# Scores of a pair in one stretch of three couples, with the norm steps of later groups half a group sooner

## The chip, the cores and the metric

The kernel runs on one core of a Trainium2 chip. The metric is the device time of one launch in microseconds (us). A program on one core is compared here by the median of several runs, beside one profiled execution.

## The reference

Attention with RMS-normed queries and keys for 8 batches of 12 heads, 448 tokens and 64 channels a head, followed by a token mixer of rank 32 and a feed-forward block of 768 to 3072 to 768 channels.

```python
q_n, k_n = rmsnorm(q, g_q), rmsnorm(k, g_k)              # over the 64 channels
scores = q_n @ k_n.T / 8                                 # 448 x 448 for each head
attn = softmax(scores)
x = attn @ v                                             # heads side by side: 448 x 768
u = x + (x.T @ U @ V).T                                  # U 448 x 32, V 32 x 448
out = u + relu(u @ w_ch1) @ w_ch2
```

## The kernel before

**Units.** Two heads make a pair, and each batch has six pairs. Two pairs make a group `gi`; there are 24 groups, three to a batch. In a group the first pair is `a == 0` and the second is `a == 1`; `pr` is the pair's number in its batch, and `pairs[i]` lists all 48.

**Norm of a group.** `load` brings q, k and v to SBUF (SP's queue). `squares` (ScalarE, or GpSimd for the early groups) and `sums` (VectorE, two reductions) give the sums of squares; `roots` (ScalarE, lines 169 and 170, `Ln` and `Exp`) gives the factors; `scale_dma` (GpSimd) multiplies, and `values` (GpSimd) casts v. `roots`, the scaling and `values` together are `scale_all`. From group 6 on (`DMA_FROM`, the third batch, as batches count from 0) `turn_dma` turns q and k by four DMA transposes on SP's queue, and `take_dma` multiplies the turned q by the gains on GpSimd (line 386). The buffer of the turned groups is double.

**Scores of a pair.** `Sc(b, pr, r)` with r = 0, 1, 2 computes 128 keys for both heads of the pair: two matmuls that contract 64 rows each, one in the upper and one in the lower half of the array, which run side by side (a couple). Their results are two PSUM banks of one tile of the pool `ps_sc` (2 tiles of 2 banks). r = 3 takes the last 64 keys of both heads in one matmul over 128 rows, whose result is a tile of the pool `ps` (4 tiles of one bank). ScalarE's `Exp` (line 416) takes each result to `E`, of which there are two. `Srows` issues several of them back to back, which is called a stretch here. From the third batch a group had three stretches of two couples: (0, 1) of its first pair; (2) of the first and (0) of the second, then r = 3 of the first; (1, 2) of the second, then r = 3.

**Values of a pair.** `V(b, pr, half)` multiplies `E` by v into a tile `pv` of the pool `ps`; VectorE divides by the sum (lines 444 and 445).

**Mixer and feed-forward.** `mix_t`, `mix_tr` and eight `mix_rows` for each batch; then 24 `up` pieces (6 matmuls each, line 529, emptied by ScalarE's `Relu`, line 536), then `down` in parts of 6 matmuls (line 561); four parts fill one tile `po`, which VectorE empties (line 571). All of these take their PSUM tile from the pool `ps` too, so `ps` serves `ph1`, `po`, `pv`, `pu`, `pw`, `pm` and r = 3 of the scores.

**Order.** The order on every engine is the order in which the program issues, and it is written out by a planner. It has two lists: `att` (attention pieces, each with a cost) and `mlp` (mixer and feed-forward pieces, each with a cost; `up` 1.14, a `down` part 0.98). `ca` and `cm` are the costs issued so far. An attention piece is issued once `ca` is not above `due(cm)`, which is linear in pieces; otherwise the next `mlp` piece is issued:

```python
take_att = ia < len(att) and (not may_mlp or ca <= due(cm) and ready(*att[ia][1:]))
return a_two + (a_all - a_two) * (c - SECOND) / (m_end - m_one - SECOND)
```

So a step of cost 0 (`squares`, `sums`, `scale_all`, `turn_dma`, `take_dma`, `load`) is issued together with the next step behind it that costs something, and not with the one ahead of it. `m_one` is the cost of the `mlp` list up to its first piece of the second batch.

Of the kernel before, what the change touches and what calls it, by code (L numbers as in the profile page):

```python
# [9 lines left out]
FP32 = mybir.dt.float32  # L10
BF16 = mybir.dt.bfloat16
AX = mybir.AxisListType.X
AF = mybir.ActivationFunctionType
# [6 lines left out]
DMA_FROM = 6  # L20
# [6 lines left out]
def kernel(  # L27
# [13 lines left out]
    nc = tc.nc  # L41
    B, H, S, D = q.shape
# [4 lines left out]
    P = 128  # L47
    NT = S // 64
    NJ = S // P
    SM = NJ * P  # L50
# [8 lines left out]
    NPAIR = H // 2  # L59
    HALF = dm // 2  # L60
    scal = 1.0 / (D ** 0.5)
# [6 lines left out]
    ep = ctx.enter_context(tc.tile_pool(name="ep", bufs=2))  # L68
    xp = ctx.enter_context(tc.tile_pool(name="xp", bufs=3))
    outp = ctx.enter_context(tc.tile_pool(name="outp", bufs=3))  # L70
    ps_sc = ctx.enter_context(tc.tile_pool(name="ps_sc", bufs=2, space=bass.MemoryType.PSUM))
    ps = ctx.enter_context(tc.tile_pool(name="ps", bufs=4, space=bass.MemoryType.PSUM))


    groups = []
# [183 lines left out]
    bias = gg[:, 1:2]  # L259
# [77 lines left out]
    at = {"pe": 0.0, "act": 0.0, "dve": 0.0}  # L337
    exp_done = {}

    def runs(eng, us):  # L340
        at[eng] = us + (at["pe"] if eng == "pe" else max(at["pe"], at[eng]))

    qk, es, xs = {}, {}, {}
# [57 lines left out]
    NB = 2 * NJ + 1  # L401

    def Sc(b, pr, r):
        qT, kT = qk[divmod(b * NPAIR + pr, 2)]
        if r == 0:
            es[(b, pr)] = ep.tile([P, NB, S], BF16, name="E", tag="E")
        n = min(2, NB - 2 * r)
        if r < NJ or b == 0:
            sc = ps_sc.tile([P, 2, 512], FP32, name="sc", tag="sc")
        else:  # L410
            sc = ps.tile([P, 1, 512], FP32, name="sl", tag="ps")
        keys = slice(r * P, (r + 1) * P)
        for i in range(n):
            d = slice(i * D, (i + 1) * D) if r < NJ else slice(0, P)
            nc.tensor.matmul(sc[:, i, :S], kT[d, keys], qT[d], start=True, stop=True)  # L415
        nc.scalar.activation(es[(b, pr)][:, 2 * r:2 * r + n, :], sc[:, :n, :S], AF.Exp, scale=scal, bias=bias)  # L416
        runs("pe", 0.25)
        runs("act", 0.9 if n == 2 else 0.52)
        exp_done[(b, pr)] = at["act"]

    def Srows(blocks):
        for x in blocks:
            Sc(*x)
# [158 lines left out]
    pairs = [(b, pr) for b in range(B) for pr in range(NPAIR)]  # L582
    att = []

    def add_att(cost, f, *a):
        att.append((cost, f, a))
# [58 lines left out]
    for i, (b, pr) in enumerate(pairs):  # L645
        if b == 0:
            continue
        gi, a = divmod(i, 2)
        more = gi + 1 < len(groups)
        by_dma = gi + 1 >= DMA_FROM  # L650
        soon = gi + 2 < len(groups)

        if a == 0:
            if pr == 0 and b > 1:
                add_att(0.5, V, *pairs[i - 1], 0)
                add_att(0.5, V, *pairs[i - 1], 1)
            add_att(0.45, Srows, ((b, pr, 0), (b, pr, 1)))
            if gi == DMA_FROM:
                add_att(0.0, sums, gi + 1, 0)
                add_att(0.0, sums, gi + 1, 1)  # L660
                add_att(0.0, load, gi + 2)
            if by_dma and more and gi >= DMA_FROM:
                add_att(0.0, scale_all, gi + 1)
            if b == 1 and pr == 0:
                add_att(0.8, lambda: None)
            if not by_dma:
                add_att(0.0, squares, gi + 1, 0, nc.gpsimd)
                add_att(0.0, squares, gi + 1, 1, nc.gpsimd)
                if gi + 2 < DMA_FROM:
                    add_att(0.0, load, gi + 3)  # L670
            if pr != 0:
                add_att(0.4, V, *pairs[i - 1], 0)
                add_att(0.5, V, *pairs[i - 1], 1)
            if gi < DMA_FROM:
                add_att(0.0, sums, gi + 1, 0)
                add_att(0.0, sums, gi + 1, 1)
            add_att(1.0, Srows, ((b, pr, 2), (b, pr + 1, 0), (b, pr, 3)))
            if more and gi + 1 > DMA_FROM:
                add_att(0.0, turn_dma, gi + 1)
                add_att(0.0, take_dma, gi + 1)  # L680
                if gi + 3 < len(groups):
                    add_att(0.0, load, gi + 3)
            if gi < DMA_FROM:
                add_att(0.0, scale_all, gi + 1)
            if gi + 2 == DMA_FROM:
                add_att(0.0, squares, gi + 2, 0, nc.gpsimd)
                add_att(0.0, squares, gi + 2, 1, nc.gpsimd)
                add_att(0.0, weights, 2)
            add_att(0.4, V, b, pr, 0)
        else:  # L690
            add_att(0.6, Srows, ((b, pr, 1), (b, pr, 2), (b, pr, 3)))
            if not by_dma:
                add_att(0.5, V, *pairs[i - 1], 1)
                add_att(0.39, T, gi + 1, 0)
                add_att(0.39, T, gi + 1, 1)
                continue
            if gi + 1 == DMA_FROM:
                add_att(0.5, V, *pairs[i - 1], 1)
                add_att(0.0, turn_dma, gi + 1)
                add_att(0.0, load, gi + 2)  # L700
                add_att(0.0, take_dma, gi + 1)
                add_att(0.0, squares, gi + 2, 0, nc.gpsimd)
                add_att(0.0, squares, gi + 2, 1, nc.gpsimd)
                continue
            if soon:
                add_att(0.0, squares, gi + 2, 0)
                add_att(0.0, squares, gi + 2, 1)
            add_att(0.5, V, *pairs[i - 1], 1)
            if soon:
                add_att(0.0, sums, gi + 2, 0)  # L710
                add_att(0.0, sums, gi + 2, 1)
    add_att(0.55, V, *pairs[-1], 0)
    add_att(0.55, V, *pairs[-1], 1)

# [9 lines left out]
    for b in range(B):  # L724
# [14 lines left out]
        tiles = [(col, half) for col in cols for half in range(2)]  # L739
# [81 lines left out]
    while ia < len(att) or im < len(mlp):  # L821
# [8 lines left out]
        if take_att:  # L830
            c, f, a = att[ia]
# [11 lines left out]
        else:  # L843
            c, f, a, _ = mlp[im]
# [34 lines left out]
```

## Time and profile before

| what | value |
|---|---|
| median of 3 runs (lowest, highest) | 591.55 us (589.73, 592.12) |
| own time of the profiled execution | 590.86 us |
| its span | 589.0 us |
| TensorE matmul busy | 575.1 us, 4825 instructions |
| ScalarE busy | 300.2 us |
| VectorE busy | 197.1 us |
| GpSimd busy | 213.8 us |
| `Exp` of a couple, 128x896 | 1003 ns, x144 |
| `Exp` of r = 3, 128x448 | 638 ns, x42 |
| `Relu` of an `up`, 128x448 | 548 ns |
| one reduction of `sums` | 1079 ns |

The profiled execution took 1.9 us more than its span and 0.7 us less than the median. In a row of the timeline, the first number is the start in us from the span's start, the second how long the group of instructions took from its first start to its last end; matmuls overlap, so the distance from one start to the next is what TensorE spends. What stands in square brackets is idle time of that engine ahead of the row, and what ended it.

### The profile page before, as it was taken

What the parts mean: (1) busy time and instruction counts of PE and PEld (TensorE: products, weight loads), DVE (VectorE), ACT (ScalarE), POOL (GpSimd) and SP (SyncE); (2) the same over time, 40 slices, a digit from 0 to 9 for tenths busy, and PEclk for the clock granted to TensorE, in tenths of its full rate; (3) what the DMA queues carried; (4) which work ended last, traced back from release to release, by engine and by line L of the source; (5) the groups of instructions that cost most, each with busy time, mean ns of one, the idle gap of its engine ahead of it and who ended that gap; (6) DMA issues with size and microseconds to landing.
All of it is one profiled execution on the core that took longest, in us unless ns stands there. A gap on an engine that the chain in (4) does not pass through costs nothing.

```text
span 589.0 us, 11701 instructions
## 1 busy us (share of the span) xinstructions
PE 575.1 (98%) x4825; PEld 335.0 (57%) x4826; DVE 197.1 (33%) x458; ACT 300.2 (51%) x472; POOL 213.8 (36%) x312
## 2 busy tenths in 40 slices
PE   8899999989999999999999999999999999999996
PEld 7555556545665555555566555665556655655563
DVE  6576655312344223521244320631134310410011
ACT  6866750668453774466753568347753254014200
POOL 4995684373144434415054605333352000000000
PEclk9999999999999999999999999999999999999999
DMA  8799997773636651674166732567014210420022
GB/s 217 164 241 241 241 200 186 180 170 99 145 67 165 156 127 18 169 198 107 22 155 100 190 96 37 158 161 155 9 37 105 48 28 1 61 67 1 1 53 55
DMA packets 104509, 68.21 MB, mean 116 GB/s; under 512 B 66568, under 2 KB 101256, under 8 KB 104456
## 3 DMA queue, kind: packets, MB, share of 16 engines
q1 hardware_dynamic: 95044, 58.03, 41.7%
q0 software_dynamic: 9408, 9.44, 9.6%
q8 instruction: 38, 0.62, 0.4%
q14 instruction: 15, 0.12, 0.1%
q10 hardware_dynamic: 4, 0.00, 0.0%
HBM read 52.20 MB, written 11.01 MB: 107 GB/s over the span
## 4 chain that ended last, share of the span: by engine, by line
PE 91%; DMA 3%; SPq 1%; POOL 1%; ACT 1%; issue 1%; DVE 1%; POOLq 0%; ACTq 0%
PE po L561 36%; PE ph L529 36%; PE pv L441 6%; PE sc L415 5%; PE sl L415 2%; PE pv L437 2%; DMA qf<-in_q_dram 2%; PE pm L512 2%; ACT E L416 1%; DMA vf<-in_v_dram 1%; PE pu L460 1%; DMA qT<-qn 1%; PE pt L354 1%; POOL kp L174 1%; SPq L100 0%
## 5 line engine op out<-in xcount | busy, mean ns | idle before, releaser
L561 PE MATMUL po<-w2b,hT 128*128 128x384 bf16 x1344 | 237.7, 326 | 0.0
L529 PE MATMUL ph<-uT,w1b 128*128 128x448 bf16 x1140 | 229.4, 352 | 0.0
L416 ACT ACTIVATE E<-sc,gg 128x896 bf16<-128x896 f32 (+1 forms) x150 | 140.1, 988 | 119.5 <-PE sc L415 119.2
L561 PEld LDWEIGHTS <-hT 128*128 128x128 bf16 x1344 | 125.9, 98 | 77.0 <-issue 3.3
L529 PEld LDWEIGHTS <-w1b 128*128 128x128 bf16 x1140 | 107.9, 98 | 95.1 <-issue 3.0
L536 ACT ACTIVATE hT<-ph 128x448 bf16<-128x448 f32 x184 | 98.4, 548 | 122.7 <-PE ph L529 121.9
L444 DVE RECIPROCAL r<-pv 128x4 f32<-128x4 f32 x96 | 17.4, 182 | 185.8 <-PE pv L441 185.6
L193 POOL TENSOR_TENSOR qn<-qf,rs 128x384 bf16<-128x384 f32 x36 | 29.9, 830 | 136.9 <-ACT rs L170 136.9
L386 POOL TENSOR_SCALAR qT<-qT,gg 128x448 bf16<-128x448 bf16 x36 | 50.5, 1402 | 73.1 <-DMA qT<-qn 54.3
L571 DVE TENSOR_TENSOR ob<-po,x 128x384 f32<-128x384 f32 x48 | 26.8, 558 | 103.3 <-PE po L561 103.1
L441 PE MATMUL pv<-va,E 128*128 128x65 bf16 x1152 | 57.1, 194 | 0.0
L441 PEld LDWEIGHTS <-E 128*128 128x128 bf16 x1152 | 50.5, 98 | 6.4
L415 PE MATMUL sc<-qT,kT 64*128 64x448 bf16 (+1 forms) x294 | 43.3, 354 | 5.9 <-ACT E L416 3.0
L162 DVE TENSOR_REDUCE ssq<-sq 128x14 f32<-128x896 f32 x45 | 46.9, 1079 | 3.7 <-ACT sq L140 3.6
L437 PE MATMUL pv<-vl,E 128*128 128x130 bf16 x192 | 42.2, 220 | 0.3 <-ACT E L416 0.2
L445 DVE TENSOR_TENSOR x<-pv,r 128x256 bf16<-128x256 f32 x96 | 40.7, 424 | 3.3
L415 PEld LDWEIGHTS <-kT 64*128 64x128 bf16 (+1 forms) x336 | 14.1, 94 | 44.4 <-issue 38.2
L517 DVE TENSOR_TENSOR x<-pm,x 128x384 bf16<-128x384 f32 x48 | 26.3, 554 | 17.3 <-PE pm L512 15.0
L193 POOL TENSOR_TENSOR kp<-kf,rs 128x384 bf16<-128x384 f32 x36 | 29.8, 828 | 0.0
L416 ACT ACTIVATE E<-sl,gg 128x448 bf16<-128x448 f32 x42 | 26.8, 638 | 0.0
L437 PEld LDWEIGHTS <-E 128*128 128x128 bf16 x192 | 18.7, 97 | 9.8 <-issue 2.0
L571 DVE TENSOR_TENSOR ob<-po,u_rest 128x384 f32<-128x384 f32 x8 | 4.5, 558 | 46.9 <-PE po L561 46.9
(93 smaller groups left out, 323.5 us busy)
## 6 DMA issues: line engine op xcount, KB each, us to landing
qf<-in_q_dram SPq DMA_DIRECT2D x23, 448.0 KB, 3.6
kf<-in_k_dram SPq DMA_DIRECT2D x23, 448.0 KB, 4.8
out_dram<-ob SPq DMA_DIRECT2D x50, 192.0 KB, 2.7
vf<-in_v_dram SPq DMA_DIRECT2D x48, 192.0 KB, 5.3
w1b<-in_moe_w_ch_dram POOLq DMA_DIRECT2D x4, 1152.0 KB, 19.8
w2b<-in_moe_w_ch_dram POOLq DMA_DIRECT2D x8, 576.0 KB, 13.2
vf<-in_v_dram SPq DMA_DIRECT2D x48, 32.0 KB, 4.6
out_dram<-ob SPq DMA_DIRECT2D x12, 96.0 KB, 3.8
```

The lines of the kernel that those rows point to most:

```text
L162: nc.vector.tensor_reduce(ssqs[gi][:, i, :], sqs.pop((gi, i)), AX, ALU.add)
L193: nc.gpsimd.tensor_tensor(main.rearrange("p (t i) d -> p i t d", i=2), src[:, c, :2 * NJ].rearrange("p (i t) d -> p i t d", i=2), rs[:, c, ...
L386: nc.gpsimd.tensor_scalar(qT[:, a], qT[:, a], gg[:, 0:1], None, ALU.mult)
L415: nc.tensor.matmul(sc[:, i, :S], kT[d, keys], qT[d], start=True, stop=True)
L416: nc.scalar.activation(es[(b, pr)][:, 2 * r:2 * r + n, :], sc[:, :n, :S], AF.Exp, scale=scal, bias=bias)
L437: nc.tensor.matmul(pv[:, i].rearrange("p e d -> p (e d)"), E[:, 2 * NJ, w:w + P], vl[:, lp, :], start=True, stop=False)
L441: nc.tensor.matmul(pv[:, i, e, :], E[:, 2 * j + e, w:w + P], va[:, (first_h + step * e) * NJ + j, :], start=False, stop=(e == 1 and j == N ...
L445: nc.vector.tensor_tensor(xs[b].rearrange("p i (h d) -> p i h d", d=D)[:, 2 * half:2 * half + 2, h0:h0 + step + 1:step, :], pv[:, :, :, :D ...
L529: nc.tensor.matmul(ph, w1b[:, dt, ht * P:(ht + 1) * P], uT[:, dt, off:off + S], start=(dt == 0), stop=(dt == KD - 1))
L536: nc.scalar.activation(hT[:, ht, off:off + S], ph, AF.Relu)
L561: nc.tensor.matmul(po, hT[:, ht, col:col + P], w2b[:, ht, half * HALF:(half + 1) * HALF], start=(ht == 0), stop=(ht == KH - 1))
L571: nc.vector.tensor_tensor(ob[:, h], po, urows(b, col, half), ALU.add)
```

## The change

From group 6 on a pair's scores are issued by a new function, `Spair`, in one stretch: the couple r = 2 first, into two one-bank tiles of `ps`, then the couples 0 and 1 into the two tiles of `ps_sc`, then r = 3 into a third tile of `ps`. The results of r = 2 have an `Exp` each. A group so has two stretches of three couples where it had three of two. Each pair is now: `Spair`, then the two `V` of the pair before it (in a batch's first pair, these two `V` and then `Spair`).

The norm steps move as well. `squares` of group gi + 2 stay ahead of the second `V` in the second pair of group gi. `sums` of gi + 2 stay behind that `V`, and now `scale_all` of gi + 2 follows them there; before, it came in the next group behind its first stretch. `turn_dma`, `take_dma` and `load` come behind the group's first stretch and no longer behind its second. Around group 6 the load of group 7 moves from behind `turn_dma` of group 6 to the group before; the squares of group 7 go from GpSimd to ScalarE, ahead of `turn_dma` of group 6; its `sums` and `scale_all` come ahead of the last `V` of the second batch.

```diff
+    def Spair(b, pr):
+        qT, kT = qk[divmod(b * NPAIR + pr, 2)]
+        E = es[(b, pr)] = ep.tile([P, NB, S], BF16, name="E", tag="E")
+        ts = [ps.tile([P, 512], FP32, name="sl", tag="ps")[:, :S] for _ in range(2)]
+        for i in range(2):
+            d = slice(i * D, (i + 1) * D)
+            nc.tensor.matmul(ts[i], kT[d, 2 * P:3 * P], qT[d], start=True, stop=True)
+        for i in range(2):
+            nc.scalar.activation(E[:, 4 + i, :], ts[i], AF.Exp, scale=scal, bias=bias)
+        ...
+        tiles = [ps_sc.tile([P, 2, 512], FP32, name="sc", tag="sc") for _ in range(2)]
+        for r in range(2):
+            for i in range(2):
+                d = slice(i * D, (i + 1) * D)
+                nc.tensor.matmul(tiles[r][:, i, :S], kT[d, r * P:(r + 1) * P], qT[d], start=True, stop=True)
+        last = ps.tile([P, 512], FP32, name="sl", tag="ps")[:, :S]
+        nc.tensor.matmul(last, kT[:, SM:], qT, start=True, stop=True)
+        nc.scalar.activation(E[:, 6, :], last, AF.Exp, scale=scal, bias=bias)
+        for r in range(2):
+            nc.scalar.activation(E[:, 2 * r:2 * r + 2, :], tiles[r][:, :, :S], AF.Exp, scale=scal, bias=bias)
...
+        if a == 0 and pr == 0 and b > 1:
+            add_att(0.5, V, *pairs[i - 1], 0)
             if gi == DMA_FROM:
                 add_att(0.0, sums, gi + 1, 0)
                 add_att(0.0, sums, gi + 1, 1)
-                add_att(0.0, load, gi + 2)
-            if by_dma and more and gi >= DMA_FROM:
                 add_att(0.0, scale_all, gi + 1)
+            add_att(0.5, V, *pairs[i - 1], 1)
+        if gi >= DMA_FROM:
+            add_att(1.0, Spair, b, pr)
+            if a == 0 and more:
+                add_att(0.0, turn_dma, gi + 1)
+                add_att(0.0, take_dma, gi + 1)
+                if gi + 3 < len(groups):
+                    add_att(0.0, load, gi + 3)
+            if pr != 0:
+                add_att(0.45, V, *pairs[i - 1], 0)
+                if a == 1 and soon:
+                    add_att(0.0, squares, gi + 2, 0)
+                    add_att(0.0, squares, gi + 2, 1)
+                add_att(0.45, V, *pairs[i - 1], 1)
+                if a == 1 and soon:
+                    add_att(0.0, sums, gi + 2, 0)
+                    add_att(0.0, sums, gi + 2, 1)
+                    add_att(0.0, scale_all, gi + 2)
+            continue
...
             add_att(0.6, Srows, ((b, pr, 1), (b, pr, 2), (b, pr, 3)))
+            if gi + 2 == DMA_FROM:
+                add_att(0.0, load, gi + 3)
...
-            if gi + 1 == DMA_FROM:
-                add_att(0.5, V, *pairs[i - 1], 1)
-                add_att(0.0, turn_dma, gi + 1)
-                add_att(0.0, load, gi + 2)
-                add_att(0.0, take_dma, gi + 1)
-                add_att(0.0, squares, gi + 2, 0, nc.gpsimd)
-                add_att(0.0, squares, gi + 2, 1, nc.gpsimd)
-                continue
...
+            add_att(0.0, squares, gi + 2, 0)
+            add_att(0.0, squares, gi + 2, 1)
             add_att(0.5, V, *pairs[i - 1], 1)
...
+            add_att(0.0, turn_dma, gi + 1)
+            add_att(0.0, take_dma, gi + 1)
+            add_att(0.0, load, gi + 3)
```

More of the change, by code (lines that the diff above doesn't have):

```diff
@@ L419, in Sc @@
         exp_done[(b, pr)] = at["act"]
+    def Spair(b, pr):
[7 more added lines that the diff above has]
+            nc.scalar.activation(E[:, 4 + i, :], ts[i], AF.Exp, scale=scal, bias=bias)
+        runs("pe", 0.4)
+        runs("act", 1.04)
+        tiles = [ps_sc.tile([P, 2, 512], FP32, name="sc", tag="sc") for _ in range(2)]
[8 more added lines that the diff above has]
+            nc.scalar.activation(E[:, 2 * r:2 * r + 2, :], tiles[r][:, :, :S], AF.Exp, scale=scal, bias=bias)
+        runs("pe", 0.6)
+        runs("act", 2.3)
+        exp_done[(b, pr)] = at["act"]
     def Srows(blocks):
@@ L651 @@
         soon = gi + 2 < len(groups)
-        if a == 0:
-            if pr == 0 and b > 1:
-                add_att(0.5, V, *pairs[i - 1], 0)
-                add_att(0.5, V, *pairs[i - 1], 1)
-            add_att(0.45, Srows, ((b, pr, 0), (b, pr, 1)))
+        if a == 0 and pr == 0 and b > 1:
+            add_att(0.5, V, *pairs[i - 1], 0)
             if gi == DMA_FROM:
@@ L660 @@
                 add_att(0.0, sums, gi + 1, 1)
-                add_att(0.0, load, gi + 2)
-            if by_dma and more and gi >= DMA_FROM:
                 add_att(0.0, scale_all, gi + 1)
-            if b == 1 and pr == 0:
+            add_att(0.5, V, *pairs[i - 1], 1)
[17 more added lines that the diff above has]
+            continue
+        if a == 0:
+            add_att(0.45, Srows, ((b, pr, 0), (b, pr, 1)))
+            if pr == 0:
                 add_att(0.8, lambda: None)
@@ L673 @@
                 add_att(0.5, V, *pairs[i - 1], 1)
-            if gi < DMA_FROM:
-                add_att(0.0, sums, gi + 1, 0)
-                add_att(0.0, sums, gi + 1, 1)
+            add_att(0.0, sums, gi + 1, 0)
+            add_att(0.0, sums, gi + 1, 1)
             add_att(1.0, Srows, ((b, pr, 2), (b, pr + 1, 0), (b, pr, 3)))
-            if more and gi + 1 > DMA_FROM:
-                add_att(0.0, turn_dma, gi + 1)
-                add_att(0.0, take_dma, gi + 1)
[L681 to L684, printed above, removed]
+            add_att(0.0, scale_all, gi + 1)
             if gi + 2 == DMA_FROM:
@@ L696 @@
                 continue
-            if gi + 1 == DMA_FROM:
-                add_att(0.5, V, *pairs[i - 1], 1)
-                add_att(0.0, turn_dma, gi + 1)
-                add_att(0.0, load, gi + 2)
-                add_att(0.0, take_dma, gi + 1)
-                add_att(0.0, squares, gi + 2, 0, nc.gpsimd)
-                add_att(0.0, squares, gi + 2, 1, nc.gpsimd)
-                continue
-            if soon:
-                add_att(0.0, squares, gi + 2, 0)
-                add_att(0.0, squares, gi + 2, 1)
+            add_att(0.0, squares, gi + 2, 0)
+            add_att(0.0, squares, gi + 2, 1)
             add_att(0.5, V, *pairs[i - 1], 1)
-            if soon:
-                add_att(0.0, sums, gi + 2, 0)
-                add_att(0.0, sums, gi + 2, 1)
+            add_att(0.0, turn_dma, gi + 1)
+            add_att(0.0, take_dma, gi + 1)
+            add_att(0.0, load, gi + 3)
     add_att(0.55, V, *pairs[-1], 0)
```

## The prediction

> **What bounds the kernel.** I read the page first.
>
> ```profile
> PE 575.1 (98%) x4825; PEld 335.0 (57%) x4826; DVE 197.1 (33%) x458; ACT 300.2 (51%) x472; POOL 213.8 (36%) x312
> PE 91%; DMA 3%; SPq 1%; POOL 1%; ACT 1%; issue 1%; DVE 1%; POOLq 0%; ACTq 0%
> ```
>
> TensorE is busy 98% of the span and carries 91% of the chain that ended last. No other engine is near full, so the change counts only through what TensorE spends or waits. A busy TensorE hides what a matmul really costs, so I read start-to-start distances in the timeline of TensorE next (columns: start, length, what).
>
> ```profile
> 412.96 2.43 PE L529 MATMUL ph<-uT,w1b 128*128 128x448 bf16 x12
> 415.23 0.22 PE L437 MATMUL pv<-vl,E 128*128 128x130 bf16 x1
> ...
> 415.72 2.43 PE L529 MATMUL ph<-uT,w1b 128*128 128x448 bf16 x12
> 418.08 0.55 PE L415 MATMUL sc<-qT,kT 64*128 64x448 bf16 x4
> 418.57 2.44 PE L529 MATMUL ph<-uT,w1b 128*128 128x448 bf16 x12
> 420.94 0.55 PE L415 MATMUL sc<-qT,kT 64*128 64x448 bf16 x4
> 421.43 0.36 PE L415 MATMUL sl<-qT,kT 128*128 128x448 bf16 x1
> ```
>
> Twelve `up` matmuls ahead of a `V` take 415.23 − 412.96 = 2.27 us, 0.189 each. Ahead of a stretch they take 418.08 − 415.72 = 2.36: entering the 64-row couples costs 0.09. The two couples take 418.57 − 418.08 = 0.49, where the distance inside the stretch is 0.20: leaving costs another 0.09. The twelve behind it, which end in an entry too, take 2.37: 0.01 more. So a stretch costs 0.19 us, however many couples it holds.
>
> The list of waits shows what TensorE stands idle for in score matmuls (total, times, longest):
>
> ```profile
> PE sc L415 <- ACT E L416: 3.0, 5, 1.0
> PE sc L415 <- POOL qT L386: 2.0, 1, 2.0
> ```
>
> By the timeline the five waits for `E` lie in the first 33 us, which the change doesn't touch. The single one for GpSimd is at group 7:
>
> ```profile
> 114.06 2.32 SPq L378 DMA_TRANSPOSE qT<-qn  x1
> ...
> 117.94 1.40 POOL L386 TENSOR_SCALAR qT<-qT,gg 128x448 bf16<-128x448 bf16 x1 [7.21 <-DMA qT<-qn]
> ...
> 119.39 0.55 PE L415 MATMUL sc<-qT,kT 64*128 64x448 bf16 x4 [2.01 <-POOL qT L386]
> ```
>
> From the first transpose to the end of the gain is 119.34 − 114.06 = 5.3 us. After it TensorE waits for no PSUM tile.
>
> Last, the order of `roots` and `Exp` on ScalarE, and the sizes of `Exp` by shape:
>
> ```profile
> 102.42 2.07 DVE L162 TENSOR_REDUCE ssq<-sq 128x14 f32<-128x896 f32 x2
> ...
> 104.38 0.55 PE L415 MATMUL sc<-qT,kT 64*128 64x448 bf16 x4
> 104.52 0.32 ACT L169 ACTIVATE rs<-ssq,eps 128x28 f32<-128x28 f32 x1 [0.37 <-DVE ssq L162]
> ...
> 104.87 0.23 ACT L170 ACTIVATE rs<-rs 128x28 f32<-128x28 f32 x1
> 105.01 1.89 ACT L416 ACTIVATE E<-sc,gg 128x896 bf16<-128x896 f32 x2
> ```
> ```profile
> L416 ACT ACTIVATE E<-sc,gg 128x896 bf16<-128x896 f32 x144 | 136.7, 1003 | 118.6 <-PE sc L415 118.2
> L416 ACT ACTIVATE E<-sl,gg 128x448 bf16<-128x448 f32 x42 | 26.8, 638 | 0.0
> ```
>
> Here `roots` stands ahead of the `Exp` of a stretch and waits for the two reductions; the `Exp`, whose matmuls were done at 104.75, waits behind it. It cost TensorE nothing, since these scores lay in `ps_sc`.
>
> **What is removed.** Eighteen groups lose one stretch each: 18 × 0.19 = 3.4 us. The couples stay as many.
>
> The 2.0 us at 117 should go. Now `scale_all` of group 7 is issued ahead of the last `V` of batch 1 (at 89.45 before), and the transposes behind the first `Spair` and four down parts; SP reaches them once the output of the tile just finished is issued, near 107.6. Plus 5.3 that is 113, and `Spair` of group 7 comes at about 116. Gain 2.0; if the cover of 3 us were gone, the old wait is back.
>
> **What is moved under cover.** For later groups `turn_dma` (four transposes on SP) and `take_dma` (two of 1.40 on GpSimd) lie ahead of the `Spair` that needs them by at least one `Spair`, two `V` and eight pieces, 10.7 us, against 5.3. `scale_all` is 4 × (0.83 + 0.29) + 0.82 + 0.64 = 5.9 us on GpSimd, which is 36% busy. Splitting the `Exp` of r = 2 costs ScalarE 2 × 0.52 − 0.895 = 0.15 us a pair by start distances, 5 us in all, on an engine that is 51% busy; uncovered, it would be those 5 us.
>
> The load of group 7 (3 × 448 KB = 1.34 MB) moves to a stretch where the DMA engines are full: windows give a share of 1.28 to 1.32 for 70 to 90 us, and 0.60 after. At the 203 GB/s of 80 to 85 it puts the last weights of the down projection off by 6.6 us, to about 97. TensorE needs them at 100.8. Nothing, with 4 us to spare.
>
> **What is added: a wait on ScalarE with PSUM tiles behind it.** A step of cost 0 is issued with the next one that costs something. So `sums` and `scale_all` of group gi + 2 come right ahead of the next `Spair` (ahead of a `V` where a batch begins). On ScalarE `roots` waits for two reductions on VectorE, and behind it are the five `Exp` of `Spair` and then the `Relu` of the `up` pieces. `Spair` holds three of the four tiles of `ps`, which only these `Exp` give back. In a down stretch an open `po` holds the fourth. The next piece that wants a tile waits, and TensorE with it. No row shows this wait. Its lower end is 0, as at 104.52; its upper end, the dearest case below in all eleven places where `roots` is right ahead of a `Spair`, 11 × 2.4 = 26.
>
> I take it place by place. From the costs, `due` rises 0.220 attention for each unit of `mlp` after the third batch (before: 0.223; that rule gives the order the trace shows), so one or two pieces lie between a `V` and the `Spair` behind it, and about four behind a `Spair`. `Spair` takes TensorE 0.98 (0.09 + 3 × 0.20 + 0.09 + 0.20).
>
> Batches are counted from 0. Down stretch, third pair of batch 5 (`V`, `mix_t`, first part of a new `po`, `Spair`, `mix_tr`): let T be the end of `mix_t`. VectorE copies `pu` until T + 0.54 and reduces until T + 2.6 (2.07 for both); `roots` ends at T + 3.1 (starts 0.35 apart, then 0.13); the first `Exp` (0.64) at T + 3.8. TensorE has issued the part (0.98) and `Spair` at T + 1.96 and wants a tile for `mix_tr`: 1.8 us. The same in batch 6: 1.8. In batch 4 two adds of the mixer and one of `po` (0.55 each) stand ahead of the reductions: 2.4.
>
> Up stretch with one `up` between, third pair of batch 2: let T be the start of the `V`. The `Relu` ahead, then both `squares` (0.83 apart), end at T + 2.3; reductions at T + 3.7; `roots` T + 4.2; first `Exp` T + 4.8. TensorE is through `Spair` at T + 2.6, waits 0.3 for the tile of the `up` between, whose `Relu` stands behind the squares, and 0.9 for the one after: 1.2. The same in the fifth pair of batch 4: 1.2.
>
> The other places have two pieces or more to spare, or have no `roots` ahead and ask for a tile some 0.2 before the first `Exp` ends; nine waits of 0.03 to 0.52 sum to 1.3. Together 6.0 + 2.4 + 1.3 = 9.7. The same walk through the old order gives 0, as measured.
>
> [...]
>
> **Sum.** 590.86 (the profiled execution's own time) − 3.4 − 2.0 + 9.7 = 595.2. The median of the runs was 0.7 above that execution: 595.9.
>
> **Rivals.** About 0.5%, 3 us, can be told from no change here, so slower begins at 594.5 and faster ends at 588.6.
>
> *No wait: faster.* If the reductions are done by the time `Spair` is issued, because VectorE runs ahead of TensorE, only the gains count: 586.1 by the median, up to 588.6 with small waits left. For: 67% of VectorE is free and the old order shows no such wait. Against: VectorE can't pass the copy of the `V` just ahead, and the reductions take 2.07. It decides where three pieces, not one, lie between. Chance 0.16.
>
> *Half the wait: no change.* The down places cost a third of what I say (another tile comes free first) and the up places stay: 590 to 594. Chance 0.26.
>
> *Late weights: slower still.* The load of group 7 takes the DMA engines from the weights for longer than 10 us from 65 us on, so that down parts, or the last `V` of batch 1 behind `sums` on VectorE, wait 3 to 8 us: 599 to 604. For: the share of 1.3. Against: 4 us of cover. Chance 0.06.
>
> *The forecast*, waits of 8.4 to 13: 594.5 to 599. Chance 0.52.
>
> **How the numbers follow.** Slower 0.52 + 0.06 = 0.58, same 0.26, faster 0.16. The range begins at 588, which leaves out most of the first rival (0.13 of its 0.16), and ends at 602, in the middle of the third (0.03 left out): 0.16 outside. The forecast's own range is 594.5 to 599.
>
> **What would show it.** Rows of score matmuls with x6 and three couples in 0.69 us, 36 of them from the third batch; no idle ahead of the scores of group 7; TensorE idle with releaser `ACT E` ahead of `pw`, `pm` or `ph` right behind a `Spair`, 1.8 to 2.4 us in the third pairs of batches 4, 5 and 6; ScalarE idle ahead of L169 with releaser `DVE ssq`. I am wrong if TensorE shows no such idle, if stretches still cost 0.19 more, or if idle appears between 80 and 105 us.

## The result, and the profile after

The changed kernel takes 594.98 us (median of 7 runs, 593.07 to 596.95) against 590.61 (7 runs, 589.34 to 592.12) of the kernel before on the same chip. The ratio is 1.007, with a 95% interval of 1.005 to 1.0089: slower, by 3.0 to 5.3 us. The profiled execution took 593.07 us with a span of 591.3, which makes it the quickest of the seven.

The first line gives busy time, share of the span and instructions of each engine; the second the chain that ended last; the third is the group of `roots` (busy, mean ns, then idle time of ScalarE just before it and what ended it).

```profile
PE 572.9 (97%) x4826; PEld 337.7 (57%) x4826; DVE 197.1 (33%) x458; ACT 306.4 (52%) x510; POOL 210.5 (36%) x310
PE 87%; ACT 4%; DVE 4%; DMA 2%; POOL 1%; issue 1%; SPq 0%; ACTq 0%; POOLq 0%
L169 ACT ACTIVATE rs<-ssq,eps 128x28 f32<-128x28 f32 (+1 forms) x25 | 7.9, 317 | 57.8 <-DVE ssq L162 50.7
```

TensorE's own work has shrunk by 2.2 us, and the time has grown: TensorE now waits. The chain says for whom, since ScalarE and VectorE hold 8% of it where they held 2%. ScalarE stands idle for 50.7 us ahead of `roots`, ended by the reductions (L162). In the list of waits of the kernel before (total, times, longest) that row was:

```profile
ACT rs L169 <- DVE ssq L162: 1.2, 4, 0.4
```

The list of waits of the changed kernel names the matmuls that pay:

```profile
PE pw L492 <- ACT E L429: 3.4, 2, 1.7
PE pm L537 <- ACT E L429: 2.2, 1, 2.2
...
PE ph L554 <- ACT E L429: 1.4, 2, 0.7
```

None of the three was there before. L429 is the `Exp` of r = 2 in `Spair`: a mixer or `up` matmul wants a tile of `ps`, and the next to come back is one that `Spair` holds. The timeline of the third pair of batch 5 (start, length, what, idle time ahead) shows the whole knot:

```profile
304.68 1.14 PE L586 MATMUL po<-w2b,hT 128*128 128x384 bf16 x6
304.87 0.36 DVE L487 CAST tb<-pu 128x192 bf16<-128x192 f32 x1
305.15 2.07 DVE L162 TENSOR_REDUCE ssq<-sq 128x14 f32<-128x896 f32 x2
305.75 0.36 PE L427 MATMUL sl<-qT,kT 64*128 64x448 bf16 x2
...
306.43 0.36 PE L438 MATMUL sl<-qT,kT 128*128 128x448 bf16 x1
...
307.31 0.32 ACT L169 ACTIVATE rs<-ssq,eps 128x28 f32<-128x28 f32 x1 [6.35 <-DVE ssq L162]
...
307.79 1.14 ACT L429 ACTIVATE E<-sl,gg 128x448 bf16<-128x448 f32 x2
...
308.46 0.27 PE L492 MATMUL pw<-ident,tb 128*128 128x128 bf16 x2 [1.67 <-ACT E L429]
```

The scores of r = 2 were done soon after 306.0. Their `Exp` began at 307.79, because `roots` stands ahead of it on ScalarE and waited for two reductions. TensorE stood 1.67 us.

At group 7 the wait has shrunk and not gone:

```profile
106.92 2.46 SPq L604 DMA_DIRECT2D out_dram<-ob  x4
109.49 1.21 SPq L378 DMA_TRANSPOSE qT<-qn  x1
...
112.26 1.40 POOL L386 TENSOR_SCALAR qT<-qT,gg 128x448 bf16<-128x448 bf16 x1 [8.16 <-DMA qT<-qn]
...
114.68 0.36 PE L427 MATMUL sl<-qT,kT 64*128 64x448 bf16 x2 [0.30 <-DMA kT<-kp]
```

### The profile page after: what moved, and what is told of

Read it like the earlier page. It is cut to its first block, busy times and chain, and to the rows that moved or that the text cites. A ratio compares the mean times of both kernels' runs of the same rounds, so it can differ in the third digit from the quotient of the medians.

```text
span 591.3 us, 11725 instructions
## 1 busy us (share of the span) xinstructions
PE 572.9 (97%) x4826; PEld 337.7 (57%) x4826; DVE 197.1 (33%) x458; ACT 306.4 (52%) x510; POOL 210.5 (36%) x310
## 4 chain that ended last, share of the span: by engine, by line
PE 87%; ACT 4%; DVE 4%; DMA 2%; POOL 1%; issue 1%; SPq 0%; ACTq 0%; POOLq 0%
PE po L586 36%; PE ph L554 35%; PE pv L466 5%; DVE ssq L162 2%; PE pv L462 2%; PE sc L436 2%; PE pm L537 2%; PE sl L427 1%; PE sl L438 1%; DMA kf<-in_k_dram 1%; DMA qf<-in_q_dram 1%; ACT E L429 1%; PE sc L415 1%; ACT E L416 1%; PE pu L485 1%
## 5 line engine op out<-in xcount | busy, mean ns | idle before, releaser
L561 ACT ACTIVATE hT<-ph 128x448 bf16<-128x448 f32 x184 | 97.1, 553 | 114.4 <-PE ph L554 113.8
L429 ACT ACTIVATE E<-sl,gg 128x448 bf16<-128x448 f32 x72 | 41.4, 627 | 65.3 <-PE sl L427 65.3
L441 ACT ACTIVATE E<-sc,gg 128x896 bf16<-128x896 f32 x72 | 69.0, 1023 | 0.0
L162 DVE TENSOR_REDUCE ssq<-sq 128x14 f32<-128x896 f32 x45 | 46.8, 1078 | 2.4 <-ACT sq L140 2.3
L416 ACT ACTIVATE E<-sc,gg 128x896 bf16<-128x896 f32 (+1 forms) x42 | 37.5, 951 | 3.8 <-PE sc L415 3.8
L169 ACT ACTIVATE rs<-ssq,eps 128x28 f32<-128x28 f32 (+1 forms) x25 | 7.9, 317 | 57.8 <-DVE ssq L162 50.7
L542 DVE TENSOR_TENSOR x<-pm,x 128x384 bf16<-128x384 f32 x48 | 26.3, 554 | 15.6 <-PE pm L537 13.3
L439 ACT ACTIVATE E<-sl,gg 128x448 bf16<-128x448 f32 x36 | 22.9, 637 | 0.0
```

What stands on the lines that cost most here:

```text
L162: nc.vector.tensor_reduce(ssqs[gi][:, i, :], sqs.pop((gi, i)), AX, ALU.add)
L429: nc.scalar.activation(E[:, 4 + i, :], ts[i], AF.Exp, scale=scal, bias=bias)
L441: nc.scalar.activation(E[:, 2 * r:2 * r + 2, :], tiles[r][:, :, :S], AF.Exp, scale=scal, bias=bias)
L561: nc.scalar.activation(hT[:, ht, off:off + S], ph, AF.Relu)
```

## The experiments

The theory: the loss comes from the place of `scale_all`, whose `roots` holds up the `Exp`s of `Spair` and with them the pool `ps`; without it the longer stretches and group 7 would gain. The rivals: the stretches themselves bring nothing; the wait costs only half, and something else fills the sum; the earlier load of group 7 makes weights late. Each experiment was compared with the kernel before on the same chip; three chips were used, one for the first four experiments, one for the next two and one for the last.

**`scale_all` behind `Spair`.** In the changed kernel, `scale_all` of the next group is issued right behind the `Spair` of a group's first pair, so that the `Exp`s stand ahead of `roots`.

```diff
+    def Spair_scale(b, pr, g):
+        Spair(b, pr)
+        if g is not None:
+            scale_all(g)
-            add_att(1.0, Spair, b, pr)
+            add_att(1.0, Spair_scale, b, pr, gi + 1 if a == 0 and more and gi > DMA_FROM else None)
-                    add_att(0.0, scale_all, gi + 2)
```

> The changed kernel, but scale_all of the group stands right behind the next group's first Spair instead of right ahead of it; nothing else moves. My theory (roots waits for the two reductions with the Exp of Spair queued behind it, while Spair holds three of the four PSUM tiles of ps): the waits of 1.8 to 2.4 us in batches 4, 5 and 6 and of 0.9 us in batches 2 and 4 go, waits of 0.2 to 0.3 us stay, 1.9 us in all instead of 9.7. Time 590.6 - 3.4 - 2.0 + 1.9 = 587.1 us, faster than before by 0.6%. Rival (the three tiles of ps that Spair holds are too many by themselves, wherever roots stands): the waits stay, 594 to 596 us.

Measured: 588.78 us (10 runs, 585.34 to 589.75), ratio 0.9957 [0.9938, 0.9976]. Every wait of a mixer or `up` matmul of over 0.4 us behind a `Spair` is gone. The same place as above now reads:

```profile
304.30 2.07 DVE L162 TENSOR_REDUCE ssq<-sq 128x14 f32<-128x896 f32 x2
304.90 0.36 PE L427 MATMUL sl<-qT,kT 64*128 64x448 bf16 x2
...
305.30 1.16 ACT L429 ACTIVATE E<-sl,gg 128x448 bf16<-128x448 f32 x2 [5.19 <-PE sl L427]
...
305.99 0.27 PE L497 MATMUL pw<-ident,tb 128*128 128x128 bf16 x2
```

The reductions run at the same distance ahead of `Spair`, 0.60 us; only `roots` no longer lies between, and `pw` follows r = 3 (305.58) after 0.41 us, where it took 2.03: a wait of 0.22 instead of 1.84. Seven such small waits are left, 1.5 us in all, where 1.9 were expected. But the time is 1.7 above the expected 587.1. In the profiled execution group 7 went the other way:

```profile
108.20 2.46 SPq L609 DMA_DIRECT2D out_dram<-ob  x4
110.76 1.21 SPq L378 DMA_TRANSPOSE qT<-qn  x1
...
115.39 2.79 POOL L386 TENSOR_SCALAR qT<-qT,gg 128x448 bf16<-128x448 bf16 x2 [11.01 <-DMA qT<-qn]
...
116.84 0.56 PE L427 MATMUL sl<-qT,kT 64*128 64x448 bf16 x2 [2.50 <-POOL qT L386]
```

The scores were due at the same time as in the changed kernel (the `V` ahead at 112.56 and 112.60), and the transposes began 1.27 us later. The first gain also waited longer for the first transpose: it began 4.63 us after it, and 2.77 in the changed kernel. The windows (length, busy time and count of PE, PEld, DVE, ACT, POOL, then TensorE's granted clock, DMA share, GB/s) show what came behind that pause:

```profile
116.00:118.00 2.00, 1.16 (x6) 0.30 (x5) 0.25 (x1) 0.59 (x2) 2.00 (x2) 0.68 0.51 80
118.00:120.00 2.00, 2.00 (x8) 0.82 (x7) 0.00 (x0) 1.90 (x4) 0.18 (x1) 0.50 0.95 310
120.00:122.00 2.00, 2.00 (x12) 1.04 (x11) 0.00 (x0) 1.97 (x6) 0.35 (x1) 0.97 1.06 312
```

TensorE came back at half its clock (0.68 over a stretch in which it worked only from 116.84 on, then 0.50) and, by the 0.97 of the last window, had it whole again by 120.1: 3.3 us of work at half speed, which cost about 1.6 more. The runs divide in the same way: four with a mean granted clock of 0.998 or more took 585.34 to 587.32 us, the six others 588.72 to 589.75.

**Reductions made twice.** The changed kernel, with the two reductions of `sums` repeated (the same sums, written again), so that `roots` waits some 2 us longer, as does what VectorE has behind it.

```diff
+    def sums_again(gi):
+        for i in (0, 1, 0, 1):
+            nc.vector.tensor_reduce(ssqs[gi][:, i, :], sqs[(gi, i)], AX, ALU.add)
-                    add_att(0.0, sums, gi + 2, 0)
-                    add_att(0.0, sums, gi + 2, 1)
+                    add_att(0.0, sums_again, gi + 2)
```

> The changed kernel with the two reductions of sums made twice in each group from group 8 on (2.1 us more of VectorE a group, 16 groups). My theory: VectorE is 33% busy, but roots waits for these reductions with Exp behind it, so each wait of the changed kernel grows by about 2.0 us and places that had none get one; walking the order with the profile's durations gives 30 us of waits instead of 9.7, so 615 us (608 to 620). Rival (the waits come from the length of ScalarE's own queue, and VectorE is off the path): under 597 us.

Measured: 620.89 us (4 runs, 619.9 to 621.74), ratio 1.0507 [1.0483, 1.0531]. The direction was right, and the size was 6 us over. The waits are nearly as expected, about 29 us by start-to-start distances beside group 7's (2.6 of the listed ones are for VectorE's own later work), where 30 were walked. The one ahead of `pm` in batch 4 grew from 2.17 to 4.16 and those of `pw` from 1.67 and 1.68 to 3.65 and 3.67:

```profile
254.99 0.48 PE L541 MATMUL pm<-tT,Vm 128*128 128x128 bf16 x3 [4.16 <-ACT E L433]
255.26 6.48 PE L590 MATMUL po<-w2b,hT 128*128 128x384 bf16 x24
```

The last row is what was missing: 24 down matmuls that take about 3.9 us at full clock (0.163 each, as the six from 247.58 to 248.56 in the same trace) took 6.3. The granted clock was 0.83 in the window from 252 to 254, 0.50 in the three up to 260 and 0.96 in the one from 260 to 262, so it was at 0.50 from about 253.3 to 260.2. Behind the pause of 3.65 it was 0.61 from 328 to 330 and 0.54 from 330 to 332, with 1.00 ahead of both and behind them; behind that of 3.67 it was 0.78 from 399 to 401 and 0.50 from 401 to 403. The mean over the span was 0.985. Worked out from these windows, at least 11.5 us of work (5.2, 3.4 and 2.9) ran at half speed, which cost some 5.7 of the 6 us that the forecast lacks. VectorE had room for the reductions; it is the order on ScalarE that makes them cost TensorE time.

**Group 7 alone.** The kernel before, with only the edits around group 6: load of group 7 earlier, its squares on ScalarE, its `sums` and `scale_all` ahead of the last `V` of batch 1, its turning behind the first stretch. Stretches and all other groups are as before.

```diff
+                if gi == DMA_FROM:
+                    add_att(0.0, sums, gi + 1, 0)
+                    add_att(0.0, sums, gi + 1, 1)
+                    add_att(0.0, scale_all, gi + 1)
...
+                add_att(0.0, turn_dma, gi + 1)
+                add_att(0.0, take_dma, gi + 1)
+                add_att(0.0, load, gi + 3)
```

> The kernel before with only what the change does around group 7: its load a group earlier, its squares on ScalarE, its sums and scale_all ahead of the last V of batch 1, its turn_dma behind the first stretch. Stretches and scale_all of later groups as before. My theory: the 2.0 us that TensorE waits for the turned q of group 7 go and nothing else moves, 588.6 us (0.3% faster). Rival one (the load of group 7 puts off the last weights or the V of batch 1): idle between 80 and 105 us, 591 us or more. Rival two (the wait only shifts to a later group): 590.6 us.

Measured: 587.91 us (6 runs, 586.86 to 588.67), ratio 0.9948 [0.9929, 0.9967]: 3.0 us gained where 2.0 were expected. TensorE has no wait for group 7, and none between 80 and 105 us that the kernel before doesn't have. So the earlier load doesn't make the weights late, and that rival is out.

**`scale_all` moved alone.** The kernel before, with `scale_all` right behind `sums` as in the change, and its stretches as they were, with r = 2 in `ps_sc`.

```diff
-            if by_dma and more and gi >= DMA_FROM:
+            if gi == DMA_FROM:
                 add_att(0.0, scale_all, gi + 1)
...
                 add_att(0.0, sums, gi + 2, 1)
+                add_att(0.0, scale_all, gi + 2)
```

> The kernel before with only scale_all of the later groups moved up: right behind sums, and so right ahead of the next stretch, as in the changed kernel. Stretches stay three of two couples. My theory: roots holds up the Exp of that stretch as in the changed kernel (ScalarE idle ahead of L169 with releaser DVE ssq), but these scores lie in ps_sc, so no piece lacks a PSUM tile: 0 to 1 us of waits, 590.6 to 591.6 us, no change. Rival (roots ahead of Exp costs TensorE by itself, through Exp or Relu): 5 us or more, 596 us.

Measured: 590.61 us (12 runs, 589.14 to 592.17), ratio 0.9989 [0.9969, 1.0009]: no change. The list of waits has both halves of the reason, ScalarE's wait for the reductions and what TensorE waits for in scores:

```profile
ACT rs L169 <- DVE ssq L162: 26.3, 13, 4.4
...
PE sc L415 <- POOL qT L386: 2.9, 1, 2.9
PE sc L415 <- ACT E L416: 2.8, 5, 0.9
```

ScalarE is held for 26.3 us (less than the 50.7 of the changed kernel, with a longest of 4.4) and TensorE doesn't feel it: its 2.9 is group 7's, and the five waits for `E` lie in the first 33 us, as before. No mixer, `up` or down matmul waits for an `Exp`. So the order on ScalarE alone costs nothing here; it costs something together with `Spair`'s three tiles of `ps`.

**Both ahead.** The first experiment, and group 7 turned right behind the first `Spair` instead of with the next step that costs something.

```diff
+    def Spair_scale(b, pr, g):
+        Spair(b, pr)
+        if g == DMA_FROM + 1:
+            turn_dma(g)
+            take_dma(g)
+        elif g is not None:
+            scale_all(g)
```

> scale_all right behind the next Spair, as in the run before, and the turn of group 7 (four transposes and the two gains) issued right behind the first Spair instead of four down parts later, so that on SP's queue it stands ahead of the output DMAs of the tile that these parts finish. My theory: the 2.5 us that TensorE stood idle for group 7 in the last run came from those DMAs (110.8 us for the first transpose); they now start near 107, and nothing is waited for. 590.9 - 3.4 - 2 to 3 + 1.6 = 586.1 us (585 to 587.5), faster than before by 0.8%. Rival (the transposes themselves are slow there, wherever they stand): idle of 2 us or more stays ahead of the scores of group 7, 588.8 us.

Measured: 585.57 us (6 runs, 585.03 to 586.28), ratio 0.9908 [0.9887, 0.9929]. This version beats both kernels: 5.3 us under the one before.

```profile
108.59 1.21 SPq L378 DMA_TRANSPOSE qT<-qn  x1
...
114.38 0.36 PE L427 MATMUL sl<-qT,kT 64*128 64x448 bf16 x2
```

No wait for group 7: only two output transfers (1.18 us) stood ahead of its transposes on SP. Eight small ones of 0.17 to 0.32 us by start-to-start distances, 1.9 in all, are left behind `Spair`. Beside the 3.0 that group 7 alone gained, some 2.3 are left for the longer stretches with their small waits, where −3.4 + 1.9 = −1.5 was foretold.

**r = 3 between the couples.** The version just shown, with the matmul of r = 3 between the couple r = 2 and the other two, so that TensorE enters and leaves 64-row matmuls once more in each of the 36 pairs. Work and `Exp`s are the same.

```diff
+        last = ps.tile([P, 512], FP32, name="sl", tag="ps")[:, :S]
+        nc.tensor.matmul(last, kT[:, SM:], qT, start=True, stop=True)
         tiles = [ps_sc.tile([P, 2, 512], FP32, name="sc", tag="sc") for _ in range(2)]
...
-        last = ps.tile([P, 512], FP32, name="sl", tag="ps")[:, :S]
-        nc.tensor.matmul(last, kT[:, SM:], qT, start=True, stop=True)
```

> The kernel with the turn at once, but in every Spair the 128-row matmul of r = 3 stands between the first couple and the other two: the same matmuls and tiles, one more change to the 64-row couples and back for each of 36 pairs. My theory: a change in and out costs 0.19 us by itself; 36 x 0.19 = 6.8 us, less up to 1.3 us where a piece now waits less for a tile: 5.5 to 6.8 us above the kernel with the turn at once, about 592.3 us. Rival (what a stretch costs is its first weight load or the queue, and comes once for each pair however its matmuls are ordered): within 1 us of that kernel, 586 to 587 us.

Measured: 591.33 us (12 runs, 590.64 to 592.24), ratio 1.0012 [0.9996, 1.0028], 5.8 above the version without it. In the profile all but two of the small waits are gone, about 1.6 us. 5.8 + 1.6 = 7.4 over 36 is 0.21 us for each extra stretch.

**Turning at once, `scale_all` ahead.** The changed kernel with group 7 turned at once and `scale_all` left where the change puts it. Against the version that beats both, only the place of `scale_all` differs.

```diff
+    def Spair_turn(b, pr, g):
+        Spair(b, pr)
+        if g is not None:
+            turn_dma(g)
+            take_dma(g)
-            add_att(1.0, Spair, b, pr)
+            add_att(1.0, Spair_turn, b, pr, gi + 1 if gi == DMA_FROM and a == 0 else None)
```

> The changed kernel (scale_all right ahead of Spair) with only the turn of group 7 issued right behind the first Spair. It differs from the kernel with the turn at once (585.6 us) in the place of scale_all alone. My theory: that place costs the waits of the walk, 9.7 - 1.9 = 7.8 us, so 593.4 us (592.5 to 594.5). Rival (part of what the changed kernel lost was the wait for group 7, and the place of scale_all costs half of it): 589 to 591 us.

Measured: 594.4 us (6 runs, 592.61 to 596.42), ratio 1.0074 [1.0048, 1.01], 8.8 above the version with `scale_all` behind, though on another chip. In its profile the places that the prediction listed have 2.17, 1.67 and 1.68 us again. Group 7 still waited 0.98, with its transposes begun at 111.17; so turning at once doesn't remove that wait in every execution. And the pause of 2.17, which ended at 243.93, was followed by 1.2 us of work at a clock of 1.00 and then by two windows at 0.53 and 0.62 (columns as above): the 24 down matmuls that began at 244.09 took 5.58 us, where 24 at 0.163 take 3.9.

```profile
241.00:243.00 2.00, 0.76 (x7) 0.14 (x4) 1.69 (x2) 0.22 (x1) 0.00 (x0) 1.00 0.39 86
243.00:245.00 2.00, 1.07 (x9) 0.74 (x9) 0.55 (x1) 1.97 (x6) 1.56 (x3) 1.00 0.00 0
245.00:247.00 2.00, 2.00 (x9) 0.93 (x8) 0.00 (x0) 1.72 (x2) 2.00 (x5) 0.53 0.30 49
247.00:249.00 2.00, 2.00 (x9) 1.00 (x8) 0.10 (x1) 0.00 (x0) 1.93 (x5) 0.62 0.73 237
```

## Why the prediction was right

**The stretches, −3.4: right.** A stretch of `Spair` takes 114.68 to 115.36 for its three couples, the 0.68 that was foretold as 0.69. That it is worth its price in time, and not only in rows, is shown by putting r = 3 between: 0.21 us for each stretch against 0.19. With the waits out of the way the kernel was 5.3 us faster, 2.3 more than by group 7 alone, and 5.8 came back with the extra stretch, so the rival that the stretches bring nothing is out. The 9.5 us of the next paragraph are waits for tiles to be emptied. They came from the order on ScalarE, which was 52% busy, and not from its load.

**The wait on ScalarE, +9.7: right in mechanism, place and size.** From start-to-start distances in the trace of the changed kernel (the list of waits shows some 0.17 less for most, since the matmul ahead stands in the trace with a modelled length of 0.36, where 0.20 is spent):

| place | foretold | measured |
|---|---|---|
| third pair of batch 5 (306 us) | 1.8 | 1.84 |
| third pair of batch 6 (373 us) | 1.8 | 1.85 |
| third pair of batch 4 (240 us) | 2.4 | 2.34 |
| third pair of batch 2 (116 us) | 1.2 | 0.84 |
| fifth pair of batch 4 (263 us) | 0.3 + 0.9 | 0.32 + 0.90 |
| small ones | 1.3 in nine | 1.40 in five |
| sum | 9.7 | 9.5 |

The one in batch 2 is 0.36 short; the 0.30 ahead of group 7's scores came first, which probably gave the reductions that time. The sum is closer than its parts, which is in part luck. Moving `scale_all` behind `Spair` removes all but small waits, doubling the reductions adds 2 us at each of the large ones, and moving `scale_all` alone, with the results of r = 2 in `ps_sc`, costs nothing. So both are needed, the held queue and the held tiles, and the rivals of no wait and of half of it fall. Turning at once shows what the place of `scale_all` is worth: where 9.5 − 1.9 = 7.6 was to go, the medians of the two versions differ by 8.8. Of the six runs with `scale_all` ahead, three had a mean granted clock under 0.998; the three others took 592.61 to 593.55, and their middle one is 7.5 above both ahead.

**Group 7, −2.0: the mis-sized term.** The step that failed is "SP reaches them once the output of the tile just finished is issued, near 107.6" and the cover of 3 us that followed. In the kernel before, 107.56 is where two output transfers begin, and they took 1.18 more. The changed kernel's profiled execution was 1.64 us ahead of the one before from the start (the same score matmul at 29.50 and 31.14), so 107.6 answers to 106.0 there, and `Spair` at "about 116" to 114.4: that one was right, its scores were due at 114.38. But SP reached the outputs only at 106.92, and there were four of them, 2.46 us; the transposes began at 109.49: 3.5 us late, which is all of the cover and 0.3 more. The wait is therefore on an edge, and it came out as 0.30, 2.50 (first experiment), 2.0 (reductions twice), 0.98 (turning at once) and 0 (group 7 alone, both ahead, and r = 3 between). The queue is not all of it: from the start of the first transpose to the first gain it took 2.77 us in the changed kernel and 2.71 with the turning at once and `scale_all` ahead, but 3.88 in the kernel before and 4.63 in the first experiment. Why it differs, and why the transposes of the feed-forward's input, ahead of the outputs on SP, begin at 101.05 in one execution and at 102.87 in another with TensorE at the same place, stays open.

**The clock: not in the sum at all.** In runs whose mean granted clock was 0.998 or more, the kernel before took 588.95 to 590.61 (10 of 21 beside the first four experiments), and in the others, down to 0.992, 590.88 to 594.25. The two versions without a pause at group 7 or a long one later, group 7 alone and both ahead, never fell below 0.998 in 12 runs, nor did r = 3 between in 12. So the long pause at group 7 seems to bring the kernel before a low clock in part of its runs (11 of 21, 9 of 17 and 2 of 11 on the three chips), for some 2 us. That would be why group 7 alone gained 3.0: against the ten runs with the clock whole it gained 1.8, where 2.0 was expected. That it is this pause was shown in the trace only for the first experiment's; the profiled execution of the kernel before kept its clock at 1.00 behind the 2.01, so for that kernel it is argued from the runs.

**The sum.** On the chip of both ahead, the kernel before has a median of 589.35 in its eight runs with the clock whole, and both ahead 585.57: 3.8 gained, where −3.4 − 2.0 + 1.9 = −3.5. For the changed kernel, −3.4 + 9.5 leaves +6.1, and +4.4 was measured (3.0 to 5.3), so group 7 and the clock together gave back 1.7, with 0.8 to 3.1 as its bounds, where the prediction had 2.0. The split between the two isn't known, and that they make up nearly what group 7 was to give is luck.

**The covers.** ScalarE is busy 6.2 us more, and nothing waits for that. No idle stands between 80 and 105 us that wasn't there before; the 4 us of spare for the weights held.

## What to carry to other kernels

Before a step is moved in an in-order queue, look at what stands behind it: here a `roots` of 0.5 us that waited for VectorE held the `Exp`s that give back PSUM, and TensorE paid 9.5 us although ScalarE was busy only 52% of the span and VectorE 33%. A step that waits for another engine belongs behind the work that frees shared tiles, not ahead of it. And of a step moved on a DMA queue, count every transfer that is issued ahead of it: here four took 2.46 us of a cover thought to be 3.

## What the runs showed of the hardware

A pause of TensorE can cost more than its length. Behind some pauses the windows show TensorE at work with a granted clock down to 0.50, and behind others it stayed at 1.00:

| run | pause of TensorE, begun at | granted clock behind it, by windows (us) |
|---|---|---|
| turning at once, `scale_all` ahead | 2.17 us, 241.8 | 0.53 (245 to 247), 0.62 (247 to 249), then 1.00 |
| first experiment | 2.50 us, 114.3 | 0.68 (116 to 118), 0.50 (118 to 120), 0.97 (120 to 122), then 1.00 |
| reductions twice | 4.16 us, 250.8 | 0.83 (252 to 254), 0.50 (254 to 260), 0.96 (260 to 262) |
| reductions twice | 3.65 us, 324.3 | 0.61 (328 to 330), 0.54 (330 to 332), then 1.00 |
| reductions twice | 3.67 us, 395.7 | 0.78 (399 to 401), 0.50 (401 to 403) |
| changed kernel | 2.17 us, 240.1 | 1.00 |
| changed kernel | 1.67 us, 306.8, and 1.68 us, 373.2 | 1.00 |
| kernel before | 2.01 us, 117.4 | 1.00 |
| `scale_all` moved alone | 2.88 us, 117.2 | 1.00 (118 to 124) |

In the changed kernel and the kernel before, every window of 10 us up to 580 us has 1.00. The length alone doesn't decide: 2.17 us is in both groups, and 2.88 kept the clock where 2.50 lost it. What does decide was not shown: these traces were taken for something else, and no run was made to test it.
